# Attention with top-routed experts on one core: the last pair of heads keeps its softmax weights in fp32

## The chip, the core and the metric

The kernel runs on one core of a Trainium2 chip. The metric is device time in microseconds (us) of one execution. Engines are named as in the profile: PE (TensorE), DVE (VectorE), ACT (ScalarE), POOL (GpSimd) and SP (SyncE, which here only issues transfers). PE's weight loads are listed apart as PEld. A line number such as L541 is a line of the kernel before.

## What is computed

An attention that keeps only scores close to the row's maximum feeds a layer of 8 experts of which each token takes one:

```python
scores = scale * np.matmul(q, k.transpose(0, 1, 3, 2))       # 8 batches, 8 heads, 576 x 576
thresh = np.max(scores, axis=-1, keepdims=True) - tau
scores = np.where(scores >= thresh, scores, -1000000000.0)
scores = scores - np.max(scores, axis=-1, keepdims=True)
attn = np.exp(scores)
attn = attn / (np.sum(attn, axis=-1, keepdims=True) + 1e-09)
x = np.matmul(attn, v)                                        # to 4608 tokens of 512
expert_idx = np.argmax(x @ w_gate, axis=1)                    # one expert of 8 for each token
for e in range(8):                                            # gate_w: the softmax of that expert
    out[mask] = gate_w[mask, None] * (np.maximum(x[mask] @ w1[e], 0.0) @ w2[e])
```

All arrays are fp32. The kernel multiplies most of them as pairs of fp16 numbers, a rounding and a remainder.

## The kernel before

**Attention.** Heads are worked on in 32 pairs, `n` = 0 to 31, four pairs to a batch. A pair has 10 steps, and in every step the work of three pairs is interleaved: scores of a coming pair for the row maximum (`s_unit`, L395 and L399, maximum on DVE), scores turned the other way for this pair (`st_unit`, L450 and L380, into `st`), and the product of the pair before with its values (`av_rest`, `av_wide`, `av_tails`). `st_unit` makes 11 tiles of weights for each pair, `t` = 0 to 10: ACT takes the exponential out of `st` into an fp32 tile, and DVE masks it with zero where the score is under the threshold.

**Two ways of a tile.** Tiles named in `WHOLE` = 6, 7, 8, 9, 10 stay fp32, and the values `vf` are fp32 too: one matmul of 65 columns (L541) for each tile and each of four blocks of 128 queries. Tiles 0 to 5 go another way: ACT rounds them to fp16 (`ph`, L488), POOL subtracts for the remainder (`pl`, L489), and for each tile and block PE makes three fp16 matmuls against the values, which `split_v` has split in the same way into `vop`: L560 with 64 columns, L561 and L562 with 65. Pairs 0 to 30 round two tiles at a time (128x1024). Pair 31 rounds one tile at a time (`single`, L492 and L493, 128x512), six on ACT and six on POOL.

**After a pair.** `evac` copies the sums from PSUM (ACT, L593 and L597), `divide` and `rounded` normalise and round them to fp16 rows `R` (L570 to L613). For pairs 0 to 30 POOL does the product (L572) and the remainder (L610), for pair 31 DVE does. SP turns each pair's rows with four transposing transfers (L663), and one more turns the 64 odd tokens of two batches (`Rh`). When a batch has all four pairs, `logits` multiplies them with the gate (`lg`), `route` finds expert and rank, and POOL sends each row to its place in DRAM (`xs`, L760).

**Experts.** 39 blocks of output rows. For each, POOL fetches rows of `xs` (L1016), SP turns them (L1022), PE multiplies with w1 into `h` (`gemm1`), ACT and DVE make `hl` of it (L1070, L1071), PE multiplies with w2 into `y` (`gemm2`), ACT scales it and POOL sends it to the output (L1122). Weights come as fp32 `wf` through SP (L955) and are split into `wb` by ACT (L972) and DVE (L975). The first blocks are started while the last batch is still in attention: the first table of places is built from the counts of six batches, the second from seven (`pc`, a matmul of counts, and some 15 small steps on DVE that end in `row`).

**Order.** Up to 16 steps before the end of attention the order on each engine is the one in which the code is written out. From there on a scheduler orders the instructions by its own model of time, so all of the last pair's products stand in its order.

**Buffers.** `ew` holds 4 tiles under the tag `e`: fp32 weights on their way to `ph` and `pl`, later `hl`.

Of the kernel before, what the change touches and what calls it, by code (L numbers as in the profile page):

```python
# [18 lines left out]
P = 128  # L19
# [34 lines left out]
def kernel(  # L54
# [196 lines left out]
    def after(k, f, where=END):  # L251
        plan(now[0] + k, f, where)
# [191 lines left out]
    def st_unit(n, t):  # L444
        d = st[n]
        w = width(t)
        sc = ps_sc.tile([P, 512], F32, tag="sc", name=f"st_{n}_{t}")
        for a, cols, rows, oc, c in blocks(t):
            q = slice(a * S + CH[c].start, a * S + CH[c].stop)
            nc.tensor.matmul(sc[rows, oc], d["KB"][a][:, cols], d["QA"][a][:, CH[c]], start=True, stop=False)  # L450
            emit(sc[rows, oc], d["CK"][a][:, cols], d["CQ"][:, q], start=False, stop=True)
        sc = sc[:, 0:w]
        if t in WHOLE:
            if t == CORNER:
                pf = pp.tile([P, w], F32, tag="pfc", name=f"e_{n}_{t}", bufs=2)
            elif "pe" in d:
                pf = d.pop("pe")[:, 1]
            else:
                d["pe"] = pp.tile([P, 2, 512], F32, tag="pf", name=f"e_{n}_{t}", bufs=3)
                pf = d["pe"][:, 0]  # L460
            d["Pf"][t] = pf
            nc.scalar.activation(pf, sc, AF.Exp, bias=ntau_f, scale=0.125 / SS)  # L462
            return lambda: masks.append(nc.vector.scalar_tensor_tensor(pf, sc, 0.0, pf, ALU.is_ge, ALU.mult).ins)
        if t == CORNER:
            pd = pf = small.tile([P, w], F32, tag="pc", name=f"e_{n}_{t}", bufs=1)
            h, l = (pp.tile([P, w], F16, tag=x, name=f"{x}_{n}_{t}", bufs=2) for x in ("phc", "plc"))
            d["Ph"][t], d["Pl"][t] = h, l
        else:
            j = int("pf" in d)
            if not j:  # L470
                d["pf"] = ew.tile([P, 2, 512], F32, tag="e", name=f"e_{n}_{t}")
                d["h"], d["l"] = (pp.tile([P, 2, 512], F16, tag=x, name=f"{x}_{n}_{t}") for x in ("ph", "pl"))
            pd, h, l = d["pf"], d["h"], d["l"]
            pf = pd[:, j]
            d["Ph"][t], d["Pl"][t] = h[:, j], l[:, j]
            if j:
                del d["pf"]
        nc.scalar.activation(pf, sc, AF.Exp, bias=ntau, scale=0.125 / SS)  # L478

        def mask():  # L480
            masks.append(nc.vector.scalar_tensor_tensor(pf, sc, 0.0, pf, ALU.is_ge, ALU.mult).ins)  # L481
            if n == NPAIR - 1 and t != CORNER:
                after(1, single, FRONT)
            elif t == CORNER or j:
                after(CASTS.get(t, 1), cast)

        def cast():
            nc.scalar.copy(h, pd)  # L488
            nc.gpsimd.tensor_tensor(l, pd, h, ALU.subtract)  # L489

        def single():
            nc.scalar.copy(h[:, j], pf)  # L492
            nc.gpsimd.tensor_tensor(l[:, j], pf, h[:, j], ALU.subtract)  # L493

        return mask

# [48 lines left out]
    def av_rest(n, a, i):  # L545
        d = st[n]
        vop, vf = vops[n % NB], vfs[n % NB]
        if "av" not in d:
            d["av"] = {}
        if i // 3 * 3 not in d["av"]:  # L550
            d["av"][i // 3 * 3] = ps_av.tile([P, 512], F32, tag="av", name=f"av_{n}_{i}")
        av = d["av"][i // 3 * 3][:, 0:6 * W].rearrange("p (i a c) -> p i a c", i=3, a=2)[:, i % 3]
        q = slice(i * P, i * P + P)
        if a == 0:
            nc.tensor.matmul(av, d["Pf"][8][:, q], vf[:, 8:10], start=i in (0, 3), stop=False)
        tvs = [tv for tv in range(NT * a, NT * a + NT) if tv not in WHOLE]
        for tv in tvs:
            last = a == 1 and i >= 2 and tv == tvs[-1]
            h, l = (d[x][tv][:, q] for x in ("Ph", "Pl"))
            nc.tensor.matmul(av[:, a, 0:D], h, vop[:, tv, W:W + D], start=False, stop=False)  # L560
            nc.tensor.matmul(av[:, a], l, vop[:, tv, 0:W], start=False, stop=False)  # L561
            nc.tensor.matmul(av[:, a], h, vop[:, tv, 0:W], start=False, stop=last)  # L562
        if a and i in (2, 3):
            after(1, lambda: evac(n, i), FRONT)
# [593 lines left out]
    for n in range(NPAIR):  # L1158

        k = NSTEP * (n - 1) - LEAD - SL  # L1160
        if n >= 2:
            plan(max(first, k - LL), lambda n=n: load_qk(n))
        if n > 1:
            plan(max(first + 1, k - TUNE["sp0"]) if n > 2 else first + 1, lambda n=n: split(n))
        if n:
            plan(max(first + 3, k) if n > 1 else first + 2, lambda n=n: stack(n))
        plan(NSTEP * n + TUNE["sv"], lambda n=n: split_v(n))
        if n:
            plan(max(first, NSTEP * n + TUNE["lv"]), lambda n=n: load_v(n))

# [317 lines left out]
```

## Time and profile before

| what | value |
| --- | --- |
| median of 3 runs | 926.7 us |
| all runs | 927.29, 922.56, 926.7 us |
| the profiled execution, its own time | 911.92 us |
| its span, first to last instruction | 910.2 us |
| mean granted PE clock | 0.997 |
| PE busy | 872.8 us, 96% |
| DVE, ACT, POOL busy | 638.2, 614.6, 547.1 us |

The profiled execution took 911.92 us, 14.8 us less than the median of the runs without a profile. Attention fills the span to about 515 us, the experts the rest. Matmul records are pipelined: one lasts from its start to a modelled end, and the next can begin long before, so the cost of a matmul in a run is read from start to start, not from its duration. An idle time in square brackets stands before the row's first instruction, with what released it. A fp32 matmul leaves two records, so x4 in an fp32 row are two matmuls of the program.

### The profile page before, as it was taken

How to read it: one execution, taken by the hardware profiler on the slowest of the kernel's cores; microseconds unless marked ns; L12 is line 12 of the kernel's file. 1: busy time of each engine (PE TensorE's matmuls, PEld its weight loads, DVE VectorE, ACT ScalarE, POOL GpSimd, SP SyncE). 2: the span in 40 equal slices, each digit the busy share in tenths (PEclk: the TensorE clock that was granted, in tenths of full speed). 3: DMA queues.
4: the chain of work that ended last, by engine and by line, in shares of the span. 5: the costliest groups of instructions: out<-in, count | busy, mean ns of one | idle time of the engine just before them, and what ended most of it. 6: DMA issues, size and time to landing. Idle time of an engine off the chain costs nothing.

```text
span 910.2 us, 25378 instructions
## 1 busy us (share of the span) xinstructions
PE 872.8 (96%) x10047; PEld 626.9 (69%) x10047; DVE 638.2 (70%) x1322; ACT 614.6 (68%) x1074; POOL 547.1 (60%) x471
## 2 busy tenths in 40 slices
PE   4899999999999999999999999999999999999996
PEld 1377777777777677777777867676666666667773
DVE  7999999989899899898988746745334251524551
ACT  4799999989999899999889624453334252433561
POOL 7578888998989889989889634323222122221132
PEclk9999999999999999999999999999999999999999
DMA  8555666666866767867457785999755664646540
GB/s 198 142 126 124 152 145 150 163 160 144 202 149 166 161 149 167 170 149 187 110 146 191 190 193 181 314 302 339 189 174 160 185 190 144 192 146 218 188 168 27
DMA packets 176981, 158.16 MB, mean 174 GB/s; under 512 B 133273, under 2 KB 149147, under 8 KB 176860
## 3 DMA queue, kind: packets, MB, share of 16 engines
q1 hardware_dynamic: 156028, 105.39, 45.8%
q0 software_dynamic: 8992, 29.18, 10.2%
q10 hardware_dynamic: 11840, 21.94, 9.0%
q8 instruction: 80, 1.31, 0.6%
q14 instruction: 41, 0.34, 0.1%
HBM read 90.56 MB, written 19.17 MB: 121 GB/s over the span
## 4 chain that ended last, share of the span: by engine, by line
PE 36%; issue 5%; DMA 5%; POOL 4%; DVE 2%; ACT 2%; SPq 1%; ACTq 0%; POOLq 0%; DVEq 0%
PE h L380 16%; PE y L380 15%; DMA out_dram<-o,gt 2%; DMA xs<-R,posi 1%; POOL out_dram L1122 1%; DMA vf<-in_v_dram 1%; SPq L663 1%; DMA wf<-in_w_dram 1%; POOL xs L760 1%; POOL pl L493 1%; PE st L450 1%; PE s L395 1%; PE s L399 1%; PE st L380 1%; POOL xn L572 0%
## 5 line engine op out<-in xcount | busy, mean ns | idle before, releaser
L489 POOL TENSOR_TENSOR pl<-e,ph 128x1024 f16<-128x1024 f32 x93 | 198.6, 2136 | 51.3 <-ACT ph L488 45.4
L411 DVE TENSOR_REDUCE nm<-s 128x1 f32<-128x512 f32 (+1 forms) x320 | 199.9, 634 | 9.5 <-PE s L399 7.9
L380 PE MATMUL y<-wb,hl 128*128 128x512 f16 (+2 forms) x1104 | 196.3, 347 | 0.9 <-DVE hl L1071 0.8
L380 PEld LDWEIGHTS <-wb 128*128 128x128 f16 x2304 | 182.9, 98 | 19.7 <-issue 1.5
L975 DVE SCALAR_TENSOR_TENSOR wb<-wf,wb 128x1024 f16<-128x1024 f32 x96 | 119.4, 1276 | 73.5 <-ACT wb L972 70.7
L380 PE MATMUL h<-xT,wb 128*128 128x256 f16 (+3 forms) x1632 | 160.8, 260 | 0.3 <-issue 0.3
L380 PEld LDWEIGHTS <-hl 128*128 128x128 f16 (+2 forms) x1104 | 89.0, 98 | 98.9 <-DVE hl L1071 1.4
L481 DVE SCALAR_TENSOR_TENSOR e<-st,e 128x512 f32<-128x512 f32 x192 | 129.8, 676 | 23.4 <-ACT e L478 23.1
L395 PE MATMUL s<-QK 128*128 128x512 f16 (+3 forms) x640 | 133.1, 291 | 12.5 <-POOL QK L137 8.0
L450 PE MATMUL st<-QK 128*128 128x512 f16 (+3 forms) x640 | 136.0, 288 | 4.2 <-DVE e L481 2.0
L972 ACT ACTIVATE wb<-wf 128x1024 f16<-128x1024 f32 x96 | 98.3, 1053 | 60.0 <-DMA wf<-in_w_dram 46.7
L399 PE MATMUL s<-ck,CQ 128*128 128x512 f16 (+3 forms) x640 | 137.4, 290 | 0.0
L478 ACT ACTIVATE e<-st,ntau 128x512 f32<-128x512 f32 x192 | 132.3, 692 | 7.3 <-PE st L380 3.9
L1122 POOL DMA_INDIRECT out_dram<-o,gt x39 | 44.6, 1143 | 147.3 <-ACT o L1119 138.5
L380 PE MATMUL st<-CQ,ck 128*128 128x512 f16 (+3 forms) x640 | 131.1, 286 | 1.1 <-DMA CQ<-ptT 1.0
L541 PEld LDWEIGHTS av<-vf,e 128*128 128x128 f32 x512 | 91.8, 190 | 19.6
L462 ACT ACTIVATE e<-st,ntau_f 128x512 f32<-128x512 f32 (+1 forms) x160 | 92.3, 608 | 13.8 <-PE st L380 9.5
L488 ACT CAST ph<-e 128x1024 f16<-128x1024 f32 x93 | 96.6, 1038 | 5.9 <-issue 3.2
L1070 ACT ACTIVATE hl<-h 128x512 f16<-128x512 f32 (+2 forms) x78 | 43.6, 573 | 80.6 <-PE h L380 78.5
L561 PE MATMUL av<-vop,pl 128*128 128x65 f16 x768 | 97.2, 194 | 0.5 <-issue 0.5
L560 PE MATMUL av<-vop,ph 128*128 128x64 f16 x768 | 97.0, 193 | 0.3 <-issue 0.3
L562 PE MATMUL av<-vop,ph 128*128 128x65 f16 x768 | 96.0, 193 | 0.7 <-issue 0.7
(234 smaller groups left out, 1538.0 us busy)
## 6 DMA issues: line engine op xcount, KB each, us to landing
wf<-in_w_dram SPq DMA_DIRECT2D x96, 512.0 KB
QK<-z SPq DMA_DIRECT2D x124, 144.0 KB
qkf<-in_qk_dram ACTq DMA_DIRECT2D x29, 576.0 KB
vf<-in_v_dram SPq DMA_DIRECT2D x31, 320.0 KB
ck<-z SPq DMA_DIRECT2D x62, 72.0 KB
CQ<-z ACTq DMA_DIRECT2D x58, 72.0 KB
xT<-R SPq DMA_TRANSPOSE x153
x<-in_qk_dram SPq DMA_DIRECT2D x6, 288.0 KB
```

The source lines that it names most:

```text
L380: x = nc.tensor.matmul(*a, **kw).ins
L395: nc.tensor.matmul(sc[rows, oc], d["QA"][a][:, cols], d["KB"][a][:, CH[c]], start=True, stop=False)
L399: nc.tensor.matmul(sc[rows, oc], d["CQ"][:, at:at + cols.stop - cols.start], d["CK"][a][:, CH[c]], start=False, stop=True,)
L411: nc.vector.tensor_reduce(o, sc[:, 0:width(t)], axis=AX.X, op=ALU.max, negate=True)
L450: nc.tensor.matmul(sc[rows, oc], d["KB"][a][:, cols], d["QA"][a][:, CH[c]], start=True, stop=False)
L478: nc.scalar.activation(pf, sc, AF.Exp, bias=ntau, scale=0.125 / SS)
L481: masks.append(nc.vector.scalar_tensor_tensor(pf, sc, 0.0, pf, ALU.is_ge, ALU.mult).ins)
L489: nc.gpsimd.tensor_tensor(l, pd, h, ALU.subtract)
L560: nc.tensor.matmul(av[:, a, 0:D], h, vop[:, tv, W:W + D], start=False, stop=False)
L561: nc.tensor.matmul(av[:, a], l, vop[:, tv, 0:W], start=False, stop=False)
L972: high = nc.scalar.activation(o[:, :, 0], x, AF.Copy, scale=SW)
L975: low = nc.vector.scalar_tensor_tensor(o[:, :, 1], x, SW, o[:, :, 0], ALU.mult, ALU.subtract)
```

## The change

For pair 31 every tile takes the way of `WHOLE`. Tiles 0 to 5 use three tiles of the tag `e` of `ew`, which they used before as well, and hold them until the last product with the values. `single` is gone, and so is the split of pair 31's values (`split_v`). In `av_rest`, a tile that is found among the fp32 ones is multiplied once with fp32 values in place of three times in fp16.

```diff
-        if t in WHOLE:
+        if t in WHOLE or n == NPAIR - 1:
...
-                d["pe"] = pp.tile([P, 2, 512], F32, tag="pf", name=f"e_{n}_{t}", bufs=3)
+                if t in WHOLE:
+                    d["pe"] = pp.tile([P, 2, 512], F32, tag="pf", name=f"e_{n}_{t}", bufs=3)
+                else:
+                    d["pe"] = ew.tile([P, 2, 512], F32, tag="e", name=f"e_{n}_{t}")
...
-            if n == NPAIR - 1 and t != CORNER:
-                after(1, single, FRONT)
-            elif t == CORNER or j:
+            if j:
                 after(CASTS.get(t, 1), cast)
...
-        def single():
-            nc.scalar.copy(h[:, j], pf)
-            nc.gpsimd.tensor_tensor(l[:, j], pf, h[:, j], ALU.subtract)
...
             last = a == 1 and i >= 2 and tv == tvs[-1]
+            if tv in d["Pf"]:
+                nc.tensor.matmul(av[:, a], d["Pf"][tv][:, q], vf[:, tv], start=False, stop=last)
+                continue
...
-        plan(NSTEP * n + TUNE["sv"], lambda n=n: split_v(n))
+        if n < NPAIR - 1:
+            plan(NSTEP * n + TUNE["sv"], lambda n=n: split_v(n))
```

Three places of the order. Numbers at the end of a name count tiles. On PE, the first products of pair 31 with its values; `h_1` is the second half of the first expert block, `ph_0`, `pl_0` and `e_0` are pair 31's tiles 0 and 1. Before:

```order
L380 LDWEIGHTS wb_0_9203
L380 MATMUL h_1_10420<-xTm_9829,wb_0_9203 128x128
L555 MATMUL av_0_10373<-vf_112,e_8_10162 128x130
L560 LDWEIGHTS ph_0_10032
L560 MATMUL av_0_10373<-vop_109,ph_0_10032 128x64
L561 LDWEIGHTS pl_0_10033
L561 MATMUL av_0_10373<-vop_109,pl_0_10033 128x65
L562 LDWEIGHTS ph_0_10032
L562 MATMUL av_0_10373<-vop_109,ph_0_10032 128x65
```

and after:

```order
L380 LDWEIGHTS wb_0_9203
L380 MATMUL h_1_10382<-xTm_9829,wb_0_9203 128x128
L547 MATMUL av_0_10351<-vf_112,e_8_10152 128x130
L552 MATMUL av_0_10351<-vf_112,e_0_10031 128x65 x2
L552 MATMUL av_0_10351<-vf_112,e_2_10062 128x65 x2
```

Four fp32 matmuls stand where twelve fp16 matmuls stood, with the same neighbours.

On POOL, the stretch in which it made pair 31's remainders; `xn_10026` and `xn_10319` (after: `xn_10297`) are the normalised rows of pairs 29 and 30, `xs<-R_194` the four sends of batch 6. Before:

```order
L572 TENSOR_TENSOR xn_10026<-y_10025,rs_10024 128x512
L493 TENSOR_TENSOR pl_0_10033<-e_0_10031,ph_0_10032 128x512 x2
L493 TENSOR_TENSOR pl_2_10068<-e_2_10066,ph_2_10067 128x512
L1036 TENSOR_TENSOR gt_0_10044<-Rm_10040,badi_9701 128x1
L493 TENSOR_TENSOR pl_2_10068<-e_2_10066,ph_2_10067 128x512
L610 TENSOR_TENSOR R_195<-xn_10026,R_195 128x4x128
L493 TENSOR_TENSOR pl_4_10232<-e_4_10230,ph_4_10231 128x512 x2
L572 TENSOR_TENSOR xn_10319<-y_10318,rs_10317 128x512
L760 DMA xs<-R_194,posi_10132 36864x514 x4
L610 TENSOR_TENSOR R_195<-xn_10319,R_195 128x4x128
```

and after:

```order
L567 TENSOR_TENSOR xn_10026<-y_10025,rs_10024 128x512
L1011 DMA Rm_10038<-xs,row_9703 128x514
L605 TENSOR_TENSOR R_195<-xn_10026,R_195 128x4x128
L1031 TENSOR_TENSOR gt_0_10042<-Rm_10038,badi_9701 128x1
L755 DMA xs<-R_194,posi_10124 36864x514 x4
L567 TENSOR_TENSOR xn_10297<-y_10296,rs_10295 128x512
L605 TENSOR_TENSOR R_195<-xn_10297,R_195 128x4x128
```

Six subtractions are gone, and pair 30's product moved from ahead of the four sends to behind them.

On ACT, from the first splits of expert 0's w2 to the copy of pair 31's sums (`y_10585`, after: `y_10519`). Before:

```order
L728 ACTIVATE R_194<-sm_10130 128x4
L613 CAST R_195<-xn_10319 128x4x128
L1070 ACTIVATE hl_0_10417<-h_1_10420 128x512
L972 ACTIVATE wb_0_9204<-wf_3_1_10210 128x2x512
L593 COPY y_10585<-av_0_10373 128x390
```

and after:

```order
L723 ACTIVATE R_194<-sm_10122 128x4
L967 ACTIVATE wb_0_9204<-wf_3_1_10195 128x2x512
L1065 ACTIVATE hl_0_10379<-h_1_10382 128x512
L608 CAST R_195<-xn_10297 128x4x128
L588 COPY y_10519<-av_0_10351 128x390
```

The fourth split, which waits for a load, moved ahead of the cast of `h_1` and of the cast of pair 30's rows.

## Rows read from the trace of the kernel before

**Rows 1.** Windows: each engine's busy us (instructions), granted clock, DMA share, GB/s.
```profile
520.00:540.00 20.00, 18.31 (x192) 11.59 (x190) 12.17 (x39) 6.73 (x15) 6.91 (x9) 1.00 0.72 163
...
700.00:800.00 100.00, 100.00 (x684) 66.67 (x683) 36.83 (x48) 37.78 (x49) 21.21 (x28) 1.00 0.59 182
```
**Rows 2.** Timeline of PE, idles of 490 to 570: start, duration, what, [idle before, releaser].
```profile
490.85 0.49 PE L555 MATMUL av<-vf,e 128*128 128x130 f32 x2 [1.07 <-ACT y L593]
...
532.73 0.36 PE L380 MATMUL lg<-wg,xT 128*128 128x16 f16 x8 [1.48 <-DMA xT<-Rh]
...
540.27 0.19 PE L380 MATMUL rk<-oh,before 128*128 128x40 f16 x1 [0.48 <-DVE run L712]
...
549.38 2.24 PE L380 MATMUL h<-R,wb 128*128 128x128 f16 x37 [0.44 <-DVE wb L975]
...
554.50 0.61 PE L380 MATMUL y<-wb,hl 128*128 128x512 f16 x2 [0.18 <-ACT hl L1070]
555.88 4.49 PE L380 MATMUL y<-wb,hl 128*128 128x512 f16 x20 [0.77 <-DVE hl L1071]
```
**Rows 3.** Timeline of PE, products with values, 474.9 to 520.6.
```profile
474.99 0.33 PE L541 MATMUL av<-vf,e 128*128 128x65 f32 x2
475.16 0.38 PE L395 MATMUL s<-QK 128*128 128x512 f16 x1
...
507.94 0.44 PE L555 MATMUL av<-vf,e 128*128 128x130 f32 x2
508.22 0.19 PE L560 MATMUL av<-vop,ph 128*128 128x64 f16 x1
...
508.58 0.83 PE L380 MATMUL h<-xTm,wb 128*128 128x128 f16 x12
...
514.46 0.61 PE L541 MATMUL av<-vf,e 128*128 128x65 f32 x4
514.91 0.19 PE L560 MATMUL av<-vop,ph 128*128 128x64 f16 x1
...
515.09 3.51 PE L380 MATMUL h<-xTm,wb 128*128 128x128 f16 x60
...
520.38 0.17 PE L380 MATMUL pc<-run,ones 128*128 128x8 f16 x1
```
**Rows 4.** Timeline of POOL, 500 to 528.
```profile
500.68 3.39 POOL L493 TENSOR_TENSOR pl<-e,ph 128x512 f16<-128x512 f32 x3
...
505.27 1.16 POOL L610 TENSOR_TENSOR R<-xn,R 128x512 f16<-128x512 f32 x1
...
516.45 1.18 POOL L610 TENSOR_TENSOR R<-xn,R 128x512 f16<-128x512 f32 x1
527.87 1.79 POOL L1016 DMA_INDIRECT R<-xs,row  x1 [10.24 <-DVE row L795]
```
**Rows 5.** Timeline of SP's queue, 504 to 545.
```profile
504.34 6.71 SPq L663 DMA_TRANSPOSE xT<-R  x4
511.15 2.22 SPq L955 DMA_DIRECT2D wf<-in_w_dram  x3
...
517.65 10.87 SPq L663 DMA_TRANSPOSE xT<-R  x8
...
540.89 3.59 SPq L955 DMA_DIRECT2D wf<-in_w_dram  x5
```
**Rows 6.** Timelines of ACT and DVE around the last pair's sums, 515 to 525.
```profile
515.41 1.06 ACT L972 ACTIVATE wb<-wf 128x1024 f16<-128x1024 f32 x1 [4.04 <-DMA wf<-in_w_dram]
516.37 0.47 ACT L593 COPY y<-av 128x390 f32<-128x390 f32 x1
...
516.50 2.22 DVE L975 SCALAR_TENSOR_TENSOR wb<-wf,wb 128x1024 f16<-128x1024 f32 x1 [2.88 <-ACT wb L972]
518.64 0.18 DVE L571 RECIPROCAL rs<-rs 128x6 f32<-128x6 f32 x1
...
524.20 0.17 DVE L1199 TENSOR_TENSOR pc<-pc,more 128x8 f32<-128x8 f32 x1
```

More of the change, by code (lines that the diff above doesn't have):

```diff
@@ L463, in st_unit @@
             return lambda: masks.append(nc.vector.scalar_tensor_tensor(pf, sc, 0.0, pf, ALU.is_ge, ALU.mult).ins)
[L464 to L477, printed above, removed]
+        j = int("pf" in d)
+        if not j:
+            d["pf"] = ew.tile([P, 2, 512], F32, tag="e", name=f"e_{n}_{t}")
+            d["h"], d["l"] = (pp.tile([P, 2, 512], F16, tag=x, name=f"{x}_{n}_{t}") for x in ("ph", "pl"))
+        pd, h, l = d["pf"], d["h"], d["l"]
+        pf = pd[:, j]
+        d["Ph"][t], d["Pl"][t] = h[:, j], l[:, j]
+        if j:
+            del d["pf"]
         nc.scalar.activation(pf, sc, AF.Exp, bias=ntau, scale=0.125 / SS)
@@ L481, in mask @@
             masks.append(nc.vector.scalar_tensor_tensor(pf, sc, 0.0, pf, ALU.is_ge, ALU.mult).ins)
-            if n == NPAIR - 1 and t != CORNER:
-                after(1, single, FRONT)
-            elif t == CORNER or j:
+            if j:
                 after(CASTS.get(t, 1), cast)
```

## Prediction

> **What bounds the kernel now.** I began with the busy shares by stretch of time. Deep in the experts PE is busy without a gap [rows 1], and its work there does not change, so the end moves by exactly as much as the moment moves at which PE leaves the handover from attention to experts, 490 to 570. From 520 to 540, in the middle of the handover, PE loses 1.69 us of 20 [rows 1]. Two things count, then: PE's own added work, and its idle times in the handover.
>
> Second, PE's timeline there. [rows 2] has the idles one by one. The first, 1.07 at 490.85, lies ahead of the last pair's products. The five later ones sum to 1.48 + 0.48 + 0.44 + 0.18 + 0.77 = 3.35. An idle is counted from the modelled end of the matmul before it. Eight small matmuls take 0.36 at 532.73 and one small one lasts about 0.19 at 540.27 [rows 2], so starts lie some 0.02 apart and each idle hides up to 0.15 more: 3.35 + 5 x 0.14 = 4.05 is what they cost by start times.
>
> Third, what releases these idles. The first of the five waits for transposed rows of the last batch; SP turns rows without a pause from 517.65 [rows 5], and it starts as soon as POOL ends pair 30's remainder, 516.45 + 1.18 = 517.63 [rows 4]. The other four go back to one chain: DVE makes the second table and ends `row`, POOL fetches from 527.87 [rows 4], SP turns what was fetched and only then loads the next weights at 540.89 [rows 5], ACT and DVE split them, PE may go on. This chain begins with the last pair's sums. And there DVE was late: it took its reciprocal at 518.64 right behind a split of 2.22 us that began at 516.50 because ACT's part had waited 4.04 us for a load until 515.41 [rows 6].
>
> **The PE work.** Removed: 6 tiles x 4 blocks x 3 = 72 fp16 matmuls. Twelve of them stand between 508.22 and 508.58 [rows 3]: 0.030 each, 2.16 in all. Added: 24 fp32 matmuls of 65 columns. Two of them, four records, take 514.91 - 514.46 = 0.45 in the very same surroundings [rows 3]: 0.225 each, 5.40 in all. So PE has 3.24 us more. The bounds: alone ahead of a 512-column matmul such an fp32 matmul takes 475.16 - 474.99 = 0.17, which makes +1.9; the one of 130 columns takes 508.22 - 507.94 = 0.28, which makes +4.6. I take 0.225, the row with the same shape and neighbours.
>
> The Trainium skill, FP8 and Floating Point Precision, section TensorE Precision Notes, says that true fp32 takes four passes through the array. By columns alone, 4 x 65 against 194, the price would be far smaller than the rows give; but its page TensorE: Matmul & The Clock Gate, section Weight-path perf modes, says that fast weight load is not used for fp32, and the trace sides with that: twice the columns cost 0.28 against 0.225 [rows 3], so the weights set most of the price.
>
> **ACT, DVE, POOL.** ACT loses six casts of 128x512 and one rounding of values, POOL six subtractions, of which three take 3.39 [rows 4], so 6.8 us in all, and two operations on values of about 1 us each. DVE keeps every mask. None of it ends in PE's time directly: PE has no idle between 490.85 and 532.73 [rows 2], so the remainders were there in time. Nor does the 1.07 at 490.85 vanish by itself. It waits for ACT's copy of pair 29's sums; PE now does one more score tile and the gate matmuls of batch 6 ahead of that product, but those need a PSUM buffer and transposed rows that came just then. I count it as unchanged, with bounds of a gain of 1.0 and a loss of 0.5.
>
> What the relief could reach is the two chains.
>
> Transposed rows: POOL saves 6.8, but in the new order pair 30's product (about 1 us) stands behind the four sends, and the cast on ACT between product and remainder stands behind the fourth split of w2. The sends still need ranks from DVE and the gate weights from ACT. I expect pair 30's remainder to end at 517.6 give or take 1.5, so the gate matmuls are free at 532.7 give or take 1.5. PE would arrive there at 532.73 - 1.62 + 3.24 = 534.35. The idle of 1.62 is gone, and PE is 3.24 - 1.62 = 1.6 late.
>
> The table chain: the fourth split waited for a load that SP issued at 511.15 behind four transposes, of which the later ones needed POOL's remainder of pair 29 at 505.27 + 1.16 [rows 4, 5]. With the subtractions gone that remainder comes some 5 us earlier, the load with it, and the split is over when PE ends the last pair. PE ends it at 515.09 [rows 3] + 3.24 = 518.3, and the first three blocks about 1.3 before that, 517.0. ACT's copy (0.47) and a small step (0.2), then DVE's reciprocal at about 517.8, where it was 518.64: 0.8 earlier. The second half hangs on PE more directly: the table starts at 524.20 [rows 6] and needs a matmul of counts that PE ends near 520.55 [rows 3], now 523.8. So this chain moves by -0.8 to -0.4; I take -0.5. If the split stays in the way or the last sums are waited for longer, it moves with PE, up to +3.2.
>
> The four idles on this chain cost 0.62 + 0.58 + 0.32 + 0.91 = 2.43. PE, 1.6 late, walks into them and can give back at most 2.4, to -0.8; the chain allows -0.5. **Sum:** 3.24 - 1.62 - 2.1 = -0.5.
>
> Two new waits cost nothing. The fp32 tiles hold three of the four buffers `e` until the last product; the second block's `hl` takes one of them, but its matmuls stand behind the last product that reads tiles 0 to 3 in PE's own order, so the buffer is free by then. And ACT's cast of `h_1` is behind the fourth split, to be done by the time that PE starts the first `y`, behind the 60 matmuls that reach to 518.6 [rows 3], now some 3.2 later: with a load landing at or before 515.4 and 1.06 for the split [rows 6] there are 3 us to spare.
>
> **Rivals.** *Nothing comes back from the table chain.* Its second half starts from PE's last product and the count matmul, both 3.24 later, and all four idles stay; only the transposes' idle goes, or not even that where the last pair's own rows set SP's pace. For it: the counts are in PE's order. Against it: DVE stood 2.2 us in a split at just this place. Time: 911.92 + 1.6 to 3.2, at its likeliest +3.0, 914.9.
>
> *A late load makes it slower.* Pair 30's cast is now behind the split that waits for the load. If the load lands after 517 instead of 515.4, POOL's remainder ends after 519.1, and from that point each us is one more on SP's ten transposes and on PE. With a landing at 519.5 the gate matmuls start near 536, the transposes for fetched rows and the weight loads on SP's queue behind them slip too, and the PE work comes on top: +3 to +5, at its likeliest +4, 915.9. Against it: the load's queue is relieved, not loaded.
>
> *The weights cost PE less.* If fp32 were priced by columns, 66 more x 24 at 4.49 us for 20 matmuls of 512 [rows 2], 0.42 ns a column, PE would have only +0.7; all idles then bound, and the chain starts 2.5 earlier than above until DVE bounds it: about -1.7, 910.2. The 0.45 for two matmuls [rows 3] speaks against it. This is the skill's four passes taken by themselves.
>
> *The relief runs through.* POOL's 6.8 reach both chains and the idle at 490.85 goes too: +3.24 - 4.05 - 1.2 = -2.0, 909.9.
>
> **How the numbers follow.** Chances: forecast 0.60, nothing back 0.19, late load 0.08, cheap weights 0.05, relief through 0.08. The forecast is 911.92 - 0.5 = 911.4 for a profiled execution. The runs without a profile had a median 14.8 above it; carried over, 926.7 - 0.5 = 926.2. The cases reach from -2.0 to +4.0, and the median of such runs lay within a spread of 922.56 to 927.29; the ends of the range take the lower run with -1.6, 921.0, and the upper run with +3.2, 930.5, which leaves about 2 in 10 outside. A measurement of this kernel can tell 0.5%, 4.6 us, from no change. No case on the faster side reaches that by itself, only together with the spread of the runs: 0.06. On the slower side the late load and the upper bound of the PE work come to it: 0.09. Within: 0.85.
>
> **What would show it.** PE's products of the last pair: 24 fp32 matmuls at 0.22 each, and the last one ending near 518. The idle ahead of the gate matmuls of the last batch gone, the four behind it shrunk to about 1 us in all. DVE's reciprocal for the last pair no later than 518.6 and its table starting no later than 524.2. POOL's remainder of pair 30 still near 517.6. It is wrong if PE shows a new idle between 490 and 518, if the table starts near 527, or if PE from 600 on is not what it was.

## The result, and the profile after

22 runs of each kernel in turn gave 922.01 us before (912.59 to 931.18) and 925.64 after (916.12 to 931.17). The ratio is **1.0073, 95% interval 1.0044 to 1.0101**: slower, where the sum said 0.5 us faster. Here and below, the ratios leave out executions more than 1.5% above the fastest of their own kernel, by which the widely spread kernel before loses nine of 22 (16 of 29 in experiment 5) and the changed one a single one, so the plain medians, 925.64 / 922.01 = 1.0039, should be kept beside it.

That 925.64 lies next to the forecast's 926.2 is luck. The forecast stood on a median before of 926.7, from 3 runs; 22 runs gave 922.01, and the change went the other way.

The traced executions are 12.94 us apart (911.92 and 924.86), of which the medians show 3.63, less than a third. The windows of the changed kernel, columns as in [rows 1]:

```profile
520.00:540.00 20.00, 16.68 (x175) 12.26 (x173) 11.09 (x32) 7.08 (x15) 5.57 (x9) 0.87 0.63 137
...
700.00:800.00 100.00, 100.00 (x702) 68.56 (x701) 38.35 (x50) 40.16 (x52) 22.69 (x30) 1.00 0.55 168
```

Deep in the experts PE is still busy without a gap. In the handover it lost 3.32 us of 20, not 1.69, and the granted clock was 0.87, not 1.00. PE's timeline of the changed kernel (start, duration, what, idle before and its releaser), the counterpart of [rows 2, 3]. The first row is the last score matmul of the last pair, from which both traces are counted below:

```profile
503.16 0.38 PE L380 MATMUL st<-CQ,ck 128*128 128x512 f16 x1
...
518.37 0.61 PE L533 MATMUL av<-vf,e 128*128 128x65 f32 x4
518.82 0.61 PE L552 MATMUL av<-vf,e 128*128 128x65 f32 x4
519.26 3.51 PE L380 MATMUL h<-xTm,wb 128*128 128x128 f16 x60
...
524.55 0.17 PE L380 MATMUL pc<-run,ones 128*128 128x8 f16 x1
...
527.82 3.51 PE L380 MATMUL h<-xTm,wb 128*128 128x128 f16 x60
531.63 0.44 PE L380 MATMUL h<-xTm,wb 128*128 128x128 f16 x5 [0.30 <-issue]
533.10 0.27 PE L380 MATMUL h<-xTm,wb 128*128 128x128 f16 x2 [1.03 <-issue]
533.85 0.22 PE L380 MATMUL h<-xTm,wb 128*128 128x128 f16 x1 [0.47 <-issue]
534.56 0.40 PE L380 MATMUL h<-xTm,wb 128*128 128x128 f16 x4 [0.50 <-issue]
535.98 2.72 PE L380 MATMUL h<-xTm,wb 128*128 128x128 f16 x24 [1.02 <-issue]
538.49 2.76 PE L380 MATMUL y<-wb,hl 128*128 128x512 f16 x6
541.05 1.22 PE L380 MATMUL lg<-wg,xT 128*128 128x16 f16 x40
```

The products are as forecast: the last two (four records, L552) take 519.26 - 518.82 = 0.44. The idle of 1.48 ahead of the gate matmuls is gone, and so are the four behind it. In their place stand five idles inside a block of 96 first products `h` (the matmuls of one expert block with w1), 0.30 + 1.03 + 0.47 + 0.50 + 1.02 = 3.32, whose releaser is "issue": nothing that the profile shows. Behind them TensorE was granted 1.2 GHz: six `y` matmuls take 541.05 - 538.49 = 2.56, and 1.30 in the trace of before at 2.4 GHz. From the block's start to the start of the last gate matmul 14.29 us pass; without an idle, below, it is 7.63.

The chain of the table, from the timelines of ACT, DVE and POOL, against [rows 4, 6]:

```profile
516.20 1.06 ACT L967 ACTIVATE wb<-wf 128x1024 f16<-128x1024 f32 x1 [7.46 <-DMA wf<-in_w_dram]
...
519.03 0.18 DVE L566 RECIPROCAL rs<-rs 128x6 f32<-128x6 f32 x1
...
524.76 0.17 DVE L1195 TENSOR_TENSOR pc<-pc,more 128x8 f32<-128x8 f32 x1
...
518.32 1.21 POOL L605 TENSOR_TENSOR R<-xn,R 128x512 f16<-128x512 f32 x1 [2.67 <-ACT R L608]
528.44 1.01 POOL L1011 DMA_INDIRECT R<-xs,row  x1 [8.91 <-DVE row L790]
```

The last score matmul of before:

```profile
502.49 0.38 PE L380 MATMUL st<-CQ,ck 128*128 128x512 f16 x1
```

Counted from it (502.49 before, 503.16 after), the reciprocal came 0.3 earlier, the table started 0.1 earlier, the first fetch 0.1 earlier (25.38 and 25.28). So the chain held its place, nearly as forecast, while PE's block of 96 moved from 523.64 to 527.82, 3.5 of it beyond the 0.67 by which this execution was later already. **Before, the block began 4.23 us ahead of POOL's fetches; now 0.62 ahead.** Whether that matters is what the experiments are about.

### The profile page after: what moved, and what is told of

Same layout as the page of the kernel before. It is cut to its first block, busy times and chain, and to the rows that moved or that the text cites. A ratio compares the mean times of both kernels' runs of the same rounds, so it can differ in the third digit from the quotient of the medians.

```text
span 923.1 us, 25311 instructions
## 1 busy us (share of the span) xinstructions
PE 881.4 (95%) x10023; PEld 633.8 (69%) x10023; DVE 639.3 (69%) x1322; ACT 613.4 (66%) x1067; POOL 535.8 (58%) x463
## 4 chain that ended last, share of the span: by engine, by line
PE 53%; issue 6%; DMA 3%; DVE 3%; ACT 2%; POOL 2%; SPq 1%; ACTq 0%; POOLq 0%; DVEq 0%
PE h L380 20%; PE y L380 17%; PE st L450 3%; PE st L380 2%; PE s L395 2%; PE s L399 2%; PE av L533 2%; DMA out_dram<-o,gt 2%; PE av L547 1%; DVE e L479 1%; DVE nm L411 1%; PE av L557 1%; PE av L556 1%; PE av L555 1%; POOL out_dram L1117 1%
## 5 line engine op out<-in xcount | busy, mean ns | idle before, releaser
L380 PEld LDWEIGHTS <-wb 128*128 128x128 f16 x2304 | 186.4, 99 | 25.6 <-issue 7.9
L479 DVE SCALAR_TENSOR_TENSOR e<-st,e 128x512 f32<-128x512 f32 x186 | 125.8, 676 | 22.1 <-ACT e L476 20.6
L476 ACT ACTIVATE e<-st,ntau 128x512 f32<-128x512 f32 x186 | 128.2, 692 | 7.3 <-PE st L380 3.6
L465 ACT ACTIVATE e<-st,ntau_f 128x512 f32<-128x512 f32 (+1 forms) x166 | 96.4, 612 | 15.6 <-PE st L380 11.4
L466 DVE SCALAR_TENSOR_TENSOR e<-st,e 128x512 f32<-128x512 f32 (+1 forms) x166 | 94.8, 588 | 5.7 <-ACT e L465 4.0
L556 PE MATMUL av<-vop,pl 128*128 128x65 f16 x744 | 94.6, 194 | 0.2 <-POOL pl L485 0.2
L557 PE MATMUL av<-vop,ph 128*128 128x65 f16 x744 | 93.7, 194 | 1.0 <-issue 1.0
```

What stands on the lines that cost most here:

```text
L380: x = nc.tensor.matmul(*a, **kw).ins
```

## Experiments

They ran on five chips, each kernel in turn with the kernel before.

**1. The same two kernels again, and the products' price alone** (chip 1). `casts_kept` still makes the last pair's roundings, remainders and value split, which nothing reads, in the old order:

```
+            if n == NPAIR - 1 and t not in WHOLE:
...
+                def kept():
+                    nc.scalar.copy(h[:, i], pf)
+                    nc.gpsimd.tensor_tensor(l[:, i], pf, h[:, i], ALU.subtract)
```

> The kernel before once more, timed against itself, for the scatter between executions and for a second look at its handover from attention to experts (490 to 580). Theory A (the slowdown is made by what the change adds and reorders): ratio 1.000 within 0.003, span near 910, PE clock at its upper level through the handover, PE idles of about 1 us at most. Theory B (the profiled execution of before was a lucky one: idles with no visible releaser and stretches at 1.2 GHz come and go in any kernel): ratio 1.000 as well, but this second look shows such idles and stretches at the lower level too, and a span of 915 to 925.

> The changed kernel once more. Theory A: ratio 1.006 to 1.009, and the trace again loses about 2 us more than the products' price ahead of 516, where PE waits for DVE and POOL, and again shows the idles without a releaser near 531, 562 and 573. Theory B: ratio anywhere between 1.000 and 1.010, those three idles gone or elsewhere, and the span between 911 and 923; only the products' price (about 3.2) stays.

> The changed kernel, but ACT and POOL still make the six fp16 roundings and six remainders of the last pair and still split its values; nothing reads them. PE does the 24 fp32 products. By the order of the instructions ACT, POOL, SP and PE then stand as in the kernel before, so this has the products' price alone, without the relief and without the new order. Theory A1 (the price of the products is what is lost): ratio 1.003 to 1.009, the same as the changed kernel. Theory A2 (the new order is what is lost: gate matmuls and a score tile ahead of pair 30's products, the split of w2 ahead of two casts, the sends ahead of pair 30's rows): ratio 1.000 to 1.003, because the idles at 532 and after take most of 3.2 us. The products should read 0.22 us each in either.

Measured against 915.57 (908.66 to 919.27): before again 1.0003 [0.998, 1.0026], **changed 0.9975 [0.9948, 1.0002]**, casts kept 1.001 [0.9987, 1.0033] (one of its 12 executions took 1266.0 us and is left out). The slowdown did not come back. No PE idle over 0.25 us in these three traces is without a releaser. From the last score matmul to the last product with values PE took 12.57 and 12.56 before, 15.99 changed, 15.42 with the casts kept: the products cost 3.4 as built (2.85 with the casts kept), as theory B had it, and yet the time does not grow.

**2. The kernel before without POOL's six remainders** (left out; the second product takes the rounding again with halved exponentials).

```
-            nc.gpsimd.tensor_tensor(l[:, j], pf, h[:, j], ALU.subtract)
```

> The kernel before without the six remainders that POOL makes for the last pair: the second of the three fp16 matmuls takes the rounding again in place of the remainder, and the exponential is halved to keep the sums in place, so the last pair's weights are rounded to fp16. PE has the same 72 matmuls, ACT the same casts, the order is that of the kernel before less six instructions on POOL. Relief runs through (POOL's 6.8 us stand in the chain): ratio 0.994 to 0.998. Relief is worth little (PE never waited for a remainder, and the chain hangs on DVE and loads): 0.998 to 1.001.

Measured 1.000 [0.9977, 1.0024]: relieving POOL there is worth nothing that these runs can tell, though in the trace the wait ahead of the gate matmuls is gone (the block of 96 to the last gate matmul takes 7.63). The rival that the relief runs through to both chains falls.

**3. More PE work at the same place** (chip 2), with the changed kernel a third time beside it.

```
+                for z in range(2):
+                    nc.tensor.matmul(av[:, a], d["Pf"][tv][:, q], vf[:, tv], start=False, stop=last and z == 1)
```

> The changed kernel once more, to see whether the first measurement (1.0073) or the second (0.9975) is the one that repeats. Theory A (the change itself costs time): ratio to the kernel before 1.004 to 1.009. Theory B (the change costs PE 3.4 us in the last pair, measured as 15.99 against 12.57 us from the last score matmul to the last product with values, and the handover gives it back; the rest is chance): 0.996 to 1.002, and PE from the last score matmul to the last product again 15.9 to 16.1 us. If B holds and the time is nevertheless above 1.004, its profile has PE idles without a releaser in the handover; if it is within 0.2 per cent, it has none.

> The changed kernel, with each of the 24 fp32 products of the last pair issued twice (its exponentials are halved for that, so the sums stay), which puts another 24 x 0.225 = 5.4 us on PE ahead of the handover. Theory 'paid in full' (no idle is left in the handover that more PE work could fill, since the table chain starts from PE's last product): the last score matmul to the last product takes 21.4 us and the time is 5.4 us above the changed kernel's, ratio to it 1.006. Theory 'filled again' (the handover gives back a part of any added PE work, as it gave back the first 3.4): at most 1.003 above the changed kernel. If an fp32 product costs less behind one of the same weights, the stretch is under 20 us.

The changed kernel: **0.9984 [0.9962, 1.0006]**, 912.97 against 915.25. Products twice: 917.93, 1.0054 of the changed kernel's median; the stretch took 21.35. So the first 3.4 us cost nothing and the next 5.36 cost nearly all. PE's and DVE's timelines tell why. The changed kernel:

```profile
525.27 0.17 PE L380 MATMUL pc<-run,ones 128*128 128x8 f16 x1
...
528.53 5.52 PE L380 MATMUL h<-xTm,wb 128*128 128x128 f16 x96
...
537.46 0.36 PE L380 MATMUL lg<-wg,xT 128*128 128x16 f16 x8 [1.32 <-DMA xT<-Rh]
```

With the products twice, PE, DVE and POOL:

```profile
530.04 0.17 PE L382 MATMUL pc<-run,ones 128*128 128x8 f16 x1
...
533.30 5.52 PE L382 MATMUL h<-xTm,wb 128*128 128x128 f16 x96
...
539.96 1.15 PE L382 MATMUL lg<-wg,xT 128*128 128x16 f16 x40
...
530.25 0.17 DVE L1198 TENSOR_TENSOR pc<-pc,more 128x8 f32<-128x8 f32 x1
...
533.92 1.01 POOL L1014 DMA_INDIRECT R<-xs,row  x1 [13.89 <-DVE row L793]
```

The matmul `pc` counts the tokens for the table. Before, DVE took the counts up 524.20 - 520.38 = 3.8 us after it [rows 3, 6]; in the changed kernel 0.21 after, and the same with the products twice. This slack of 3.8 in the chain is what paid for the products: 3.4 of it is spent, and from there PE's time is the chain's: the table started 530.25 - 503.28 = 26.97 after the last score matmul with the products twice, 525.48 - 503.87 = 21.61 in the changed kernel, 5.36 apart.

The kernel before does not have that slack in every execution. Its six traces show 3.82, 3.83, 3.84, 1.41, 0.78 and 0.50; the three small ones are those in which a long wait near 490 to 498 (experiment 4) had made PE late. PE and DVE in the smallest, on chip 1:

```profile
526.42 0.17 PE L380 MATMUL pc<-run,ones 128*128 128x8 f16 x1
526.92 0.17 DVE L1199 TENSOR_TENSOR pc<-pc,more 128x8 f32<-128x8 f32 x1
```

So a late PE and the added products are paid out of the same slack. What the products cost in an execution that has already spent it, no run separates. The idle for transposed rows was 1.32 in this trace of the changed kernel and 0 in the one from chip 1, where the block of 96 to the last gate matmul took 7.63.

**4. DVE's weight subtraction near 490.** Executions differ by 6 us and more before the last pair's score matmuls are over (502.49 in one trace of before, 508.53 in another). I suspected POOL's operations of holding up DVE's `wb`. One kernel makes the change for the last two pairs, one leaves out pair 30's remainders (the rounding is taken twice, exponentials halved).

```
-        if t in WHOLE or n == NPAIR - 1:
+        if t in WHOLE or n >= NPAIR - 2:
```

```
-            nc.gpsimd.tensor_tensor(l, pd, h, ALU.subtract)
+            if n < NPAIR - 2:
+                nc.gpsimd.tensor_tensor(l, pd, h, ALU.subtract)
```

> The change made for the last two pairs instead of one: pair 30 keeps its six tiles in fp32 too (in the buffers of the roundings and remainders that it no longer makes). PE gets another 24 fp32 products for 72 fp16 ones, +3.2 to +3.4 us; POOL loses three remainders of 2.1 us and two operations on values. Theory S (the stall of PE near 490 to 498 comes from DVE's subtraction for the expert weights, 1.22 us by itself, which in these traces lasted 2.2 to 6.6 us while POOL ran operations back to back): with those gone no such subtraction between 484 and 504 lasts over 2.3 us, PE's idles there, 2.6 to 6.6 in the five profiles from the second chip and the first, fall under 1.5, and the time is 0.994 to 0.999 of the kernel before. Rival (the stall has another source, or POOL's other operations hold DVE as well): the idles stay and the time is 1.002 to 1.005.

> The changed kernel without POOL's three remainders of pair 30 (left out; the products that took them take the rounding a second time, with halved exponentials, so PE's work is the same). Theory S (POOL's back-to-back operations hold up DVE's subtraction for the expert weights): the longest of these subtractions between 484 and 504 falls from 5.2 to under 3 us, PE's idles there from about 2.6 to under 1.5, and the time is 0.993 to 0.998 of the changed kernel. Rival (POOL is not what the subtraction waits for): subtractions and idles as in the changed kernel, time 0.998 to 1.002 of it.

Changed kernel, DVE's subtraction and all that POOL ran meanwhile:

```profile
491.28 5.24 DVE L970 SCALAR_TENSOR_TENSOR wb<-wf,wb 128x1024 f16<-128x1024 f32 x1
...
489.95 2.16 POOL L485 TENSOR_TENSOR pl<-e,ph 128x1024 f16<-128x1024 f32 x1
492.04 0.21 POOL L1031 TENSOR_TENSOR gt<-Rm,badi 128x1 int32<-128x1 int32 x1
492.18 1.17 POOL L605 TENSOR_TENSOR R<-xn,R 128x512 f16<-128x512 f32 x1
493.29 2.13 POOL L485 TENSOR_TENSOR pl<-e,ph 128x1024 f16<-128x1024 f32 x1
495.37 1.18 POOL L1031 TENSOR_TENSOR gt<-Rm,badi 128x1 int32<-128x1 int32 x1
```

Without pair 30's remainders, DVE, and PE behind it:

```profile
493.01 1.23 DVE L974 SCALAR_TENSOR_TENSOR wb<-wf,wb 128x1024 f16<-128x1024 f32 x1 [0.60 <-ACT wb L971]
...
498.01 0.91 PE L382 MATMUL lg<-wg,xT 128*128 128x8 f16 x28 [3.16 <-DMA xT<-R]
```

The mechanism is right: the subtraction ends 1.1 us, about its own time, after the second of POOL's remainders (493.29 + 2.13 = 495.42 and 496.52), and takes 1.23 when the remainders are not there. The Trainium skill, SBUF — State Buffer, section Who interferes with whom, says that a DVE instruction with two SBUF inputs contends with a GpSimd instruction that reads SBUF; the trace agrees, and shows that DVE waited through four POOL operations, not one. POOL's last row is the other side of it: `gt`, 0.21 at 492.04, took 1.18 at 495.37 and ended right behind the subtraction. But the gain did not come: 1.0015 [0.999, 1.0041] without the remainders, **1.0035 [1.0007, 1.0063]** with two pairs, against 0.9984 for the changed kernel. A new wait stands there, 3.16 us for transposed rows of the earlier batch in the one, 3.46 behind DVE in the other. So theory S named the mechanism and not its worth: the time with two pairs is the rival's, that without the remainders, 1.0043 of the changed kernel's median, is slower than either expected. With the chain's slack spent, another pair's products may have nothing left to pay for them; no run shows that apart.

**5. A chip of the other kind** (chip 3).

> The changed kernel again, since 1.0073 was followed by 0.9975 and 0.9984 on two other chips. Theory A (the change costs time): 1.003 to 1.009. Theory B (the change is worth nothing to -0.3 per cent, and the first ratio belongs to the chip it was taken on, whose profiles alone show PE idles without a releaser): 0.996 to 1.001 where its profile shows no such idles; above 1.003 only together with them.

> The changed kernel with one fp16 product of zeros beside each of the 24 fp32 products, so that PE has as many matmuls as before the change, and its later instructions stand where they stood before. Theory B: only their price counts, 24 x 0.030 = 0.7 us, ratio to the changed kernel 1.000 to 1.002. Rival (where the instruction stream is cut decides the idles without a releaser): if the changed kernel shows such idles on this chip and is above 1.004, this one shows fewer and is back at 1.000 to 1.002 of the kernel before.

> The changed kernel with the last pair's roundings, remainders and split of values still made, though nothing reads them: the fp32 products in the old order of ACT, POOL and SP, a second time. If the relief of ACT and POOL and the new order are worth what the first look said, this is 1.001 of the kernel before and 1.003 above the changed kernel; if that was scatter, both lie within 0.001 of each other.

```
+                nc.tensor.matmul(av[:, a], zeros, vops[0][:, tv, 0:W], start=False, stop=False)
                 nc.tensor.matmul(av[:, a], d["Pf"][tv][:, q], vf[:, tv], start=False, stop=last)
```

Here the kernel before took 912.47 to 935.15, median 927.25. Changed 1.0038 [0.9996, 1.0081] with a median of 924.99; zero products 1.0091 [1.0048, 1.0134], 927.41; casts kept 1.005 [0.9996, 1.0105], 929.58. By the plain medians the three are 0.9976, 1.0002 and 1.0025, so the ratios cannot be read here as the price of a change. All three traces have idles without a releaser. Their sums between 525 and 590 are 3.2 (an execution of 920.62), 8.6 (930.26) and 6.4 (932.36). The zero products, in PE's timeline:

```profile
531.11 3.46 PE L382 MATMUL h<-xTm,wb 128*128 128x128 f16 x59
534.76 0.44 PE L382 MATMUL h<-xTm,wb 128*128 128x128 f16 x5 [0.19 <-issue]
536.20 0.27 PE L382 MATMUL h<-xTm,wb 128*128 128x128 f16 x2 [1.00 <-issue]
...
544.81 1.15 PE L382 MATMUL lg<-wg,xT 128*128 128x16 f16 x40
```

It has as many matmuls as the kernel before and more of these idles than the changed kernel on this chip, not fewer. That speaks against the rival that the place at which the instruction stream is cut decides them, as far as one trace of each can.

**6. Has the kernel before these idles too?** Two traces fell on chip 2 again and two on a fourth chip, of the other kind (914.59 to 933.07). `fetches_apart` sets four steps between POOL's fetches:

```
-            after(1 + m, lambda m=m: fetch(NF + m))
+            after(1 + 4 * m, lambda m=m: fetch(NF + m))
```

> The kernel before, unchanged, for its trace. If the PE idles without a releaser in the handover belong to the chip and not to the change, the kernel before has them too wherever its times spread by more than 1.5 per cent: with 912 to 918 us under 1.5 us of them between 525 and 590, as in its only trace from such a chip, with 925 to 935 us 4 to 9 us of them. On a chip with times of 909 to 920 throughout it has none over 0.25 us. If the change makes them, the kernel before shows under 1.5 us at any time.

> The kernel before a second time, for a second trace from the same chip: as for the first; two traces of unequal time should differ by the idles without a releaser and the stretches at 1.2 GHz behind them, and by nothing else over 2 us.

> The changed kernel with POOL's four fetches behind the second table set apart in the planner's order (four steps between them instead of one). In the traces so far every stretch of idles without a releaser lies in or just behind a run of four to six of POOL's indirect transfers issued 0.3 us apart. Theory: such runs are what these idles go with; on a chip that shows them, the ones near 531 to 540 fall from 3 us to under 1 while those near 563 and 575, whose runs are as before, stay. Rival: they come from something else, and stay at all three places. On a chip without such idles only the price of the later fetches is seen: 1.000 to 1.004 of the changed kernel.

> The kernel before again, for its trace on a chip of the other kind, if this is one. Theory (the idles without a releaser belong to the chip): on a chip where times of the kernel before reach from 912 to over 925 us, its trace has them near 530 to 545 or 560 to 590, under 1.5 us in an execution under 918 and 4 to 9 us in one above 925. Rival (only the changed code has many of them): under 1.5 us whatever its time.

> The kernel before, a second trace from the same chip, with the same expectation: on a chip of the other kind, idles without a releaser that grow with the time of the execution; on one like the last two, none over 0.25 us.

> The changed kernel with POOL's four fetches behind the second table set apart, once more, since the last chip showed no idles without a releaser at all and could not tell. Theory (such idles go with runs of POOL's indirect transfers): on a chip that shows them, under 1 us of them near 531 to 542, where the run is broken up, and 1.5 us or more at 560 to 585. Rival: 2 to 5 us near 531 to 542 as in three of the four traces of the changed products from such chips.

On chip 2: no such idle in any of the three traces; fetches apart 0.9979 [0.9958, 1.0]; the kernel before against itself 1.0024 [1.0001, 1.0047] and 0.999. Its two traces there differ through the subtraction near 491 (6.56 us in the longer one) and waits of 1 to 4 us behind it, not through idles without a releaser, as I had expected. On the fourth chip the kernel before against itself gave 1.0004 and 1.0054 [0.9996, 1.0111], and fetches apart 1.0025 [0.9964, 1.0087]: differences as large as the one to be explained come there without any change. And there the kernel before has the idles. An execution of 917.82, PE and POOL:

```profile
524.14 5.52 PE L380 MATMUL h<-xTm,wb 128*128 128x128 f16 x96
...
533.59 0.36 PE L380 MATMUL lg<-wg,xT 128*128 128x16 f16 x8 [1.85 <-DMA xT<-Rh]
...
528.39 1.79 POOL L1016 DMA_INDIRECT R<-xs,row  x1 [10.25 <-DVE row L795]
```

One of 926.05, where a wait of 4.57 us near 497 had made PE late:

```profile
531.52 4.71 PE L380 MATMUL h<-xTm,wb 128*128 128x128 f16 x81
536.50 0.39 PE L380 MATMUL h<-xTm,wb 128*128 128x128 f16 x4 [0.26 <-issue]
537.24 0.38 PE L380 MATMUL h<-xTm,wb 128*128 128x128 f16 x4 [0.36 <-issue]
538.13 0.33 PE L380 MATMUL h<-xTm,wb 128*128 128x128 f16 x3 [0.51 <-issue]
538.88 0.22 PE L380 MATMUL h<-xTm,wb 128*128 128x128 f16 x1 [0.43 <-issue]
539.72 0.33 PE L380 MATMUL h<-xTm,wb 128*128 128x128 f16 x3 [0.62 <-issue]
540.49 1.46 PE L380 MATMUL y<-wb,hl 128*128 128x512 f16 x6 [0.44 <-issue]
...
532.70 0.98 POOL L1016 DMA_INDIRECT R<-xs,row  x1 [10.24 <-DVE row L795]
```

So the idles go with the chip, and the kernel before has them as well: 6.6 us in this execution, 1.7 in the one before it. In the early one the block of 96 starts 4.25 us ahead of the fetches and is whole; in the late one 1.18 ahead, and it is broken. All eight traces from chips of this kind fit. The table has the block's lead on POOL's first fetch, the time from the block's start to the last gate matmul (7.63 where nothing idles), and the idles without a releaser in that stretch:

| kernel, execution | lead | block to gates | idles |
|---|---|---|---|
| before, 911.92 | 4.23 | 9.27 | 0 |
| before, 917.82 | 4.25 | 9.64 | 0 |
| before, 926.05 | 1.18 | 11.24 | 2.6 |
| changed, 920.62 | 0.95 | 9.38 | 1.3 |
| changed, 924.86 | 0.62 | 14.29 | 3.3 |
| zero products, 930.26 | 0.62 | 14.68 | 3.4 |
| casts kept, 932.36 | 0.62 | 13.25 | 3.0 |
| fetches apart, 934.77 | 0.62 | 14.66 | 3.6 |

In the two rows without idles the excess over 7.63 is the wait for transposed rows, which the change was to fill. That wait falls 3 to 5 us into POOL's run, where the other rows idle, so these two cannot tell idles that were absent from idles that the wait hid. On chips of the first kind the same leads (0.62 to 0.65 in seven traces of changed kernels) go without any.

The kernel with the fetches apart was no test. Its run was not broken up, since POOL was late anyway; POOL's timeline in the execution of 934.77:

```profile
534.82 1.01 POOL L1011 DMA_INDIRECT R<-xs,row  x1 [9.05 <-DMA xT<-R]
536.13 0.96 POOL L1011 DMA_INDIRECT R<-xs,row  x1 [0.30 <-issue]
537.39 1.02 POOL L1117 DMA_INDIRECT out_dram<-o,gt  x1 [0.30 <-issue]
538.72 0.98 POOL L1011 DMA_INDIRECT Rm<-xs,row  x1 [0.31 <-issue]
540.01 0.95 POOL L1011 DMA_INDIRECT Rm<-xs,row  x1 [0.30 <-issue]
```

**7. The fetches held back behind the block** (a fifth chip).

```
+            if m == NF:
+                tc.add_manual_dep(dma.ins, mark[0].name, SYNC)
...
-            after(1 + m, lambda m=m: fetch(NF + m))
+            after(10 + m, lambda m=m: fetch(NF + m))
```

> The changed kernel with the run of fetches behind the second table held back until PE has finished the block of 96 first products that it otherwise falls upon (in the traces of the changed kernel POOL starts the run 0.62 to 0.95 us after that block's first matmul, in fast executions of the kernel before 4.2 us after it). Theory (the idles without a releaser in that block come from its meeting POOL's run of indirect transfers): on a chip that shows such idles, the block shows under 0.5 us of them instead of 3 to 7, and they turn up 3 to 6 us behind the moved start. Rival (they belong to the block of matmuls itself): the block keeps 3 to 5 us of them, though POOL issues nothing there. The fetched rows come 6 to 9 us later, so PE waits for them behind the gates: 3 to 8 us more in all. On a chip without such idles only that price is seen, 1.003 to 1.010 of the changed kernel.

1.006 [1.0029, 1.0091] on a chip without such idles, and the hold did not bite: the first fetch still started 0.62 behind the block, only its order changed, and PE waited 3.35 for ranks and 0.97 for a fetched row. This settles nothing.

## Why the prediction was wrong

**PE's work: right.** +3.24 was forecast; the stretch from the last score matmul to the last product grew from 12.57 to 15.99, +3.42. An fp32 product cost 0.22, as the row of the same shape said, not the 0.17 or 0.28 of the bounds. The last product ended near 519.3, not 518, since this execution was 0.67 later at the last score matmul already. The rival of cheap weights falls.

**The chain of the table: right in place, 0.4 off in size.** Forecast -0.5, measured -0.1 by the first fetch. The reciprocal (519.03) and the table (524.76) missed their absolute marks of 518.6 and 524.2 by less than the 0.67 by which this execution was late. What stands behind the -0.1 is that the count matmul now releases the table; the forecast had it at 523.8, with 0.4 to spare, and it came at 524.55 with 0.21. *Nothing comes back* falls with this: the chain did not move with PE by 3.2. But the load did not come earlier, as the forecast had it. Pair 29's remainder ended at 501.23 + 1.17 = 502.40, 4.0 earlier, SP issued the loads behind it at 511.15 in both traces, and ACT's split began at 516.20, later than the 515.41 of before. What gained the 0.3 at the reciprocal is that DVE's split took 1.23, not 2.22: before, it ran into POOL's remainder, which ended at 517.63, and by experiment 4 waited for it. The forecast had put all of that lateness down to the load.

**Pair 30's remainder: late, but not in the way that was feared.** ACT's split started at 516.20, 0.8 later than before, POOL's remainder ended at 518.32 + 1.21 = 519.53, past the 519.1 from which a late load was to decide, though by less than the 0.67. Yet the gate matmuls stood without a wait in this trace and with 0 to 1.3 us in the other traces of the changed kernel. The late load is not what made the first result.

**The idles: gone, and the sum fits where only they count.** On the two chips where the changed kernel was compared and idles without a releaser are absent, 0.9975 and 0.9984 stand beside the forecast's 911.4 / 911.92 = 0.9994. From the last score matmul to PE's last matmul the trace of before takes 399.67 us; the changed kernel 399.16 and 398.85 there: -0.5 and -0.8 for a forecast of -0.5. The four idles behind the gates, which were to shrink to about 1 us in all, are one of 0.76 in the first of these traces and none in the second. That is agreement, not proof: three more traces of before, from these two chips, have 395.8, 399.8 and 402.3.

**The step that failed** is "PE, 1.6 late, walks into them": it let PE come later, asked only which waits of the old trace that would fill, and put every other effect of PE's new place at nothing, without a reason. In the traces of the first measurement the new place comes with a price. The lead of 4.2 us fell to 0.62, the block met the run of fetches, and from the block to the gates it took 14.29 us instead of the 9.27 of before, with the 1.2 GHz behind the idles in it. That is 5.0 of the 12.7 by which the last matmuls of the two traces differ; 3.5 is PE's later start of the block, 3.5 came behind the gates (there before had one such idle, 0.85, and the changed kernel seven, 4.2), 0.7 was there at the last score matmul. The medians show less. A likely reason, argued from the trace of 926.05 alone, is that the kernel before meets the run too where a wait near 490 to 498 has made PE late.

**The warning stood in the numbers.** The traced execution took 911.92, the three timed ones 922.56 to 927.29, and I carried the 14.8 between them over as a constant. It was not one. The trace of before of 926.05 shows what a longer execution holds: 7.1 of its 14.1 us are there at the last score matmul (509.60 against 502.49), with DVE's subtraction at 5.08 and PE's wait of 4.57 among it, and 7.0 come later, with 6.6 of idles without a releaser against 0.85 and a stretch at 1.2 GHz from 575.9 to 582.7. A list of waits from such an execution cannot price a change that moves PE.

What was not shown: what the idles are. They come in steps of about 0.72 us, one or a few matmuls at a time, mostly 3 to 6 us into a run of POOL's indirect transfers, and only on some chips. One rival falls to the trace of the changed kernel: its larger instruction queue (80 packets, for 20046 records of PE and PEld) starts a packet at 529.4 and the next at 546.8, the other one nothing in between either, while PE stops five times between 531.3 and 536.0 and goes on each time. So these idles did not end with an instruction transfer. No run moved the fetches away from the block on such a chip, so that their meeting is the cause is argued from eight traces, not shown, and the cause stays open. Nor is it settled that the first measurement's 1.0073 is the change's at all: on such chips the kernel before came out at 1.0054 against itself, and on one of them the plain medians put the changed kernel at 0.9976.

## What to carry over

Before adding work to an engine ahead of a handover, measure the slack on the chain that starts from its result: here DVE took the counts up 3.8 us late, 3.4 us of new work were free, and the next 5.4 cost nearly full price. Measure it in more than one execution: in half of the traces of before it was 0.5 to 1.4. When the traced execution is 1 to 2% faster than the timed ones, get a second trace before reading waits from it; what it lacks is part of the kernel. And repeat a difference of half a per cent on a second chip before explaining it: here 1.0073 was followed by 0.9975, 0.9984 and 1.0038.

## What was not expected of the hardware

- PE idles without a releaser: 0.85 to 8.6 us between 525 and 590 in all eight traces from chips on which the kernel before spreads by 2% or more, none over 0.25 in the twelve from the three on which it spreads by 1.2%, one execution of 925.02 apart.
- Behind idles TensorE was granted 1.2 GHz for 3.4 to 10.2 us, but not each time. In the trace of the changed kernel there are three such stretches: 490.4 to 493.8 behind an idle of 1.40, 534.8 to 541.6 behind 0.30, 1.03, 0.47 and 0.50, and 575.8 to 579.2 behind 0.69, 0.51 and 0.50. In that of before there is none between 24 and 907, with an idle of 1.48 at 532.73, and with the fetches apart on chip 2 none between 35 and 900, with idles of 2.15, 2.12 and 2.23.
- DVE's subtraction with two SBUF inputs, 1.22 us alone, took 5.24 or 5.25 us in each trace of the changed kernel and up to 6.56 in one of before, waiting through a run of four POOL operations without a gap.
